# Cutting the last whole output store by columns, and moving two small copies between engines, at the end of a cross-network kernel

## The chip, the cores and the metric

The kernel runs on one core of one Trainium2 chip. The metric is the device time of one execution, in microseconds (us). Executions of one and the same kernel differ by up to about 0.8%, so a kernel is run several times beside the kernel before on the same chip.

## The reference, cut to what matters

```python
B, F, D, L = 16384, 26, 16, 6          # rows; Din = F * D = 416 columns; 6 layers; all bf16
def reference(x0, ws, bs):
    x = x0
    for l in range(L):
        x = x0 * (jnp.einsum('bd,de->be', x, ws[l]) + bs[l]) + x
    return x
```

## The kernel before

The 16384 rows are cut into eight groups of 2048 (groups 0 to 7). A group times a layer is a job, and a job is computed transposed: columns on the 128 partitions, rows along the free dimension. The 416 columns are three tiles of 128 and a "tail" of 32. The DMA engines turn groups 0 to 6 back with DMA transposes before storing them. The last job (group 7, last layer) is different: it is computed in natural layout, and the tile of its input that came last is turned by TensorE.

The output of groups 0 to 6 looks like this:

```python
def output(g):
    def turn(t):                                       # one 128-column tile back to row layout
        add("sp", lambda h: h.dma_start_transpose(ost[:, :, t*P:(t+1)*P], xs[s][:, t*GC:(t+1)*GC]),
            reads=[...], writes=[("ost", t)], lane="ot", batch=g)
    turn(0)
    add("sp", ... dma_start_transpose(ot3, x3s[s3]) ..., writes=["ot3"], lane="ot3", batch=g)
    add("pool", ... tensor_copy(ost[:, :, 384:416], ot3) ...)         # the "spread" of the tails
    turn(1)
    turn(2)
    add("sp", ... dma_start(out[g*GC:(g+1)*GC, :], ost) ...,          # 2048 rows of 832 B
        reads=[("ost", t) for t in range(NT + 1)], lane="out", batch=g)
```

`add` puts an instruction into an engine's queue and works out its waits from what it reads and writes. DMAs are counted on a semaphore for each `lane`. All DMAs of one lane with the same `batch` are one group: whoever waits for one of them waits until the whole group has landed (`val` below is the count at the end of the batch).

```python
for lane, batches in self.lanes.items():
    n = 0
    for k, (key, ops) in enumerate(batches):
        n += 16 * len(ops)
        for op in ops:
            total[id(op)] = (n, ops)
... group = total[id(d)][1];  val = total[id(d)][0]
```

The last job takes the rows in four parts `kk`. For each part it does matmuls (`nat_rows`, `nat_full`), a copy from PSUM by ScalarE (`nat_out`), a multiply and an add on VectorE (`nat_mul`, `nat_add`), and a store. The residual that the add needs is in `x5n`; its third tile is filled by two ScalarE copies, `turned_out(0)` and `turned_out(2)`.

Of the kernel before, what the change touches and what calls it, by code (L numbers as in the profile page):

```python
# [3 lines left out]
P = 128  # L4
# [3 lines left out]
ACT_F = mybir.ActivationFunctionType  # L8
# [13 lines left out]
class Program:  # L22
# [12 lines left out]
    def add(self, eng, fn, reads=(), writes=(), lane=None, batch=None, hold=False, release=False):  # L35
        op = Op(eng, fn, lane, batch)
        deps = {}
        if eng == "pool":
            writes = list(writes) + ["pool"]
        for t in reads:  # L40
            w = self.writer.get(t)
            if w is not None:
                deps[id(w)] = (w, True)
        for t in writes:
            w = self.writer.get(t)
            if w is not None:
                deps[id(w)] = (w, True)
            for r in self.readers.get(t, ()):
                if id(r) not in deps:
                    deps[id(r)] = (r, False)  # L50
        for d, raw in deps.values():
            if d.lane is None and d.eng == eng and lane is None and (eng == "pe" or not raw):
                continue
            op.deps.append(d)
        for t in reads:
            self.readers.setdefault(t, []).append(op)
        for t in writes:
            self.writer[t] = op
            self.readers[t] = []
        if eng == "dve":  # L60
            if hold:
                self.flush()
                self.held = op
            else:
                self.queue[eng].append(op)
                if release:
                    self.flush()
        else:
            self.queue[eng].append(op)
        if lane is not None:  # L70
            batches = self.lanes.setdefault(lane, [])
            if not batches or batches[-1][0] != batch:
                batches.append((batch, []))
            batches[-1][1].append(op)
        return op
# [123 lines left out]
def bass_standalone__cross_network_dcn__recsys_kernel(  # L199
# [6 lines left out]
    B, D = x0.shape  # L206
    L = ws.shape[0]
    NT = 3
    NJ = 4
    GC = NJ * CH  # L210
# [3 lines left out]
    LAST = NG - 1  # L214
# [29 lines left out]
    ts = [nc.alloc_sbuf_tensor(f"ts_{s}", [P, CH], BF16) for s in range(NTS)]  # L244
    ost = nc.alloc_sbuf_tensor("ost", [P, GC // P, D], BF16)
    Tb = ost[:, :, :].rearrange("p a f -> p (a f)")[:, 0:GC]
    ot3 = nc.alloc_sbuf_tensor("ot3", [P, KK, P], BF16)
# [3 lines left out]
    add = pr.add  # L251
# [21 lines left out]
    def take(n):  # L273
        got = [(ring[0] + i) % 8 for i in range(n)]
        ring[0] = (ring[0] + n) % 8
        return got
# [56 lines left out]
    free_x, free_3 = list(range(NXS)), list(range(NX3))  # L333
# [10 lines left out]
    def x3_src(g, l):  # L344
        if l == 0:
            s = slot(g)
            return x0s[s][:, XW:XW + CH], x03_toks(s)
        s = xtail[(g, l)]
        return x3s[s][:, :], [("x3", s)]
# [132 lines left out]
    def tails(batch):  # L482
# [28 lines left out]
        out=ident[:, :], in_=ident[:, :], compare_op=ALU.not_equal, fill=1.0, base=0,  # L511
# [8 lines left out]
    def load_nat(j, k0, k1):  # L520
# [6 lines left out]
        reads=["warm"], writes=["warm"])  # L527
# [18 lines left out]
    def psum_t(b):  # L546
        return psum[:, b * CH:(b + 1) * CH].bitcast(BF16)
# [72 lines left out]
    x0n7, x5n, on = (x0s[s][:, 0:XW + CH].rearrange(view, j=NJ, k=KK) for s in (sn, s5, so))  # L620
# [12 lines left out]
    def output(g):  # L633

        s, s3 = xset[(g, L)], xtail[(g, L)]
        def turn(t):
            add("sp", lambda h: h.dma_start_transpose(
                ost[:, :, t * P:(t + 1) * P], xs[s][:, t * GC:(t + 1) * GC]),
                reads=[("x", s, t, j) for j in range(NJ)], writes=[("ost", t)], lane="ot", batch=g)

        turn(0)
        add("sp", lambda h: h.dma_start_transpose(ot3[:, :, :], x3s[s3][:, :]),
            reads=[("x3", s3)], writes=["ot3"], lane="ot3", batch=g)
        add("pool", lambda h: h.tensor_copy(  # L644
            ost[:, :, NT * P:D].rearrange("p (j k) f -> p j k f", j=NJ),
            ot3[:, :, :].rearrange("p k (j f) -> p j k f", j=NJ)),
            reads=["ot3"], writes=[("ost", NT)])
        turn(1)
        turn(2)
        rows = out[g * GC:(g + 1) * GC, :]  # L650
        o = ost[:, :, :].rearrange("p (j k) f -> p j k f", j=NJ)
        pat = "(j p k) f -> p j k f" if g == 0 else "(j k p) f -> p j k f"
        add("sp", lambda h: h.dma_start(rows.rearrange(pat, j=NJ, k=KK), o),
            reads=[("ost", t) for t in range(NT + 1)], writes=[("out", g)], lane="out", batch=g)
        free_x.append(s)
        free_3.append(s3)

    x5f = x0s[s5][:, 0:XW + CH].rearrange("p (a f) -> p a f", f=D)

# [27 lines left out]
    k = 0  # L687
# [76 lines left out]
    g, l = LAST, L - 1  # L764
    src, stok = x_src(g, l)
    s3, tok3 = x3_src(g, l)
# [9 lines left out]
    def nat_full(kk, j, b, first, ts=range(NT)):  # L776
        for t in ts:
            add("pe", lambda h, t=t: h.matmul(  # L778
                bank(b, n=D), xcol(t, j, kk), wm[l][:, t, :], start=(first and t == 0),
                stop=(not first and t == NT - 1)),  # L780
                reads=[stok(t, j), ("wm", l)], writes=[("ps", b)])
# [10 lines left out]

    def turned_out(j, b):
        t = NT - 1
        add("act", lambda h: h.activation(  # L795
            x5n[:, j:j + 2, :, t * P:NT * P].rearrange("p j k f -> p (j k) f"),
            psum_t(b).rearrange("p (a f) -> p a f", f=P), ACT_F.Copy),
            reads=[("ps", b), "x5 free"], writes=[("x5n", j, t), ("x5n", j + 1, t)])

    def turn_tails(bks):  # L800
        for kk in range(KK):
# [13 lines left out]
    def nat_rows(kk, bks, first=True):  # L815
        for j in range(NJ):
            r, q = quad(g, l, j)
            add("pe", lambda h, j=j, q=q, r=r: h.matmul(  # L818
                bank(bks[j], n=D), x3col(j, kk), w3[l][q, :], start=first, stop=False, tile_position=(r * T32, 0)),
                reads=tok3 + [("w3", l, r)], writes=[("ps", bks[j])])  # L820
        for j in range(NJ):
            r, q = quad(g, l, j)
            add("pe", lambda h, j=j, q=q, r=r: h.matmul(
                bank(bks[j], n=D), ones[q, :], brow[q, :], start=False, stop=False, tile_position=(r * T32, 0)),
                reads=["ones", ("brow", r)], writes=[("ps", bks[j])])

    def nat_out(kk, j, bks):
        extra = x0_all(so) + x03_toks(so) if first_use.pop("on", None) else []
        add("act", lambda h: h.activation(on[:, j, kk, :], bank(bks[j], n=D), ACT_F.Copy),  # L829
            reads=[("ps", bks[j])], writes=extra + [("on", j, kk)])  # L830

    def nat_mul(kk, j, n=2):
        o, x0v = on[:, j:j + n, kk, :], x0n7[:, j:j + n, kk, :]
        toks = [("on", a, kk) for a in range(j, j + n)]
        add("dve", lambda h: h.tensor_tensor(o, o, x0v, ALU.mult),  # L835
            reads=toks + [("n7", a) for a in range(j, j + n)], writes=toks)

    def nat_add(kk, j, n=2):
        o, x5v = on[:, j:j + n, kk, :], x5n[:, j:j + n, kk, :]
        toks = [("on", a, kk) for a in range(j, j + n)]  # L840
        add("dve", lambda h: h.tensor_tensor(o, o, x5v, ALU.add),  # L841
            reads=toks + [("x5n", a, t) for a in range(j, j + n) for t in range(NT + 1)], writes=toks)
# [3 lines left out]
    def nat_store(kk, j0, j1, eng="sp"):  # L846
        dst = out[LAST * GC:B, :].rearrange("(j k p) f -> p j k f", j=NJ, k=KK)[:, j0:j1, kk, :]
        add(eng, lambda h: h.dma_start(dst, on[:, j0:j1, kk, :]),
            reads=[("on", j, kk) for j in range(j0, j1)],
            writes=[("out7", kk, j0)], lane=f"out7_{stores[0]}", batch=0)  # L850
        stores[0] += 1

    a0, a1, a2, a3 = bka = take(NJ)
    b0, b1, b2, b3 = take(NJ)
    bks = {0: bka, 1: [b0, b3, b1, a0], 2: [a1, a2, a3, b2], 3: [b0, b3, b1, a0]}
    for j in range(NJ):
        nat_full(0, j, bks[0][j], True, (0, 1))
    turn_tails([b0, b1, b2, b3])
    nat_rows(0, bks[0], False)
    turn_last(0, b1)  # L860
    turned_out(0, b1)
    for j in range(NJ):
        if j == 2:
            turn_last(2, b2)
        nat_full(0, j, bks[0][j], False, (2,))
        nat_out(0, j, bks[0])
    nat_mul(0, 0)
    nat_add(0, 0)
    nat_mul(0, 2)
    nat_rows(1, bks[1])  # L870
    for j in range(NJ):
        nat_full(1, j, bks[1][j], False)
        nat_out(1, j, bks[1])
        if j == 1:
            turned_out(2, b2)
            nat_mul(1, 0)
            nat_add(1, 0)
    nat_add(0, 2)
    nat_store(0, 0, NJ)
    nat_mul(1, 2)  # L880
    nat_add(1, 2)
    nat_store(1, 0, NJ)
    nat_rows(2, bks[2])
    for j in range(NJ):
# [48 lines left out]
```

## Time and profile before

| what | number | where it is read |
|---|---|---|
| time, three runs | 479.52 us (479.35 to 479.99) | times |
| TensorE busy | 98% of the span | page, part 1 |
| last add on VectorE ends | 474.3 us | timeline |
| DMA engines busy without a break (over 90% from 466.6) | 466.3 to 476.4 us | DMA view of 465 to 478 |
| end of span | 477.8 us | page |

The page of the kernel before says that TensorE is busy all the time (share of the span, and number of instructions):

```profile
PE 469.5 (98%) x3371; PEld 196.3 (41%) x3371; DVE 403.5 (84%) x695; ACT 342.9 (72%) x372; POOL 8.1 (2%) x16
```

That holds for 460 us. The last 20 us have another limit. This is the DMA view of the kernel before, in the window 465 to 478 us, cut into 40 slices of 0.325 us. The first line has the busy share of the DMA engines in tenths, the second what they moved.

```profile
DMA  0000799999999999999999999999999999920000
GB/s 0 0 0 0 271 358 348 358 351 353 343 358 305 351 353 348 338 323 353 330 340 325 340 323 338 333 330 328 330 328 341 325 343 328 320 69 3 0 0 0
DMA packets 4192, 3.41 MB, mean 262 GB/s; under 512 B 96, under 2 KB 4192, under 8 KB 4192
```

From the fifth slice on there is no gap for 10 us. The DMA engines carry 3.41 MB at their full rate, and the last byte comes about 2.4 us after the last arithmetic. Whatever makes arithmetic faster in this stretch changes nothing at the end, unless it lets the bytes start earlier.

They start when group 6 is stored. The timeline of the DMA queue (SP) in the kernel before shows start, duration of the issue, and what is issued; `x2` means two merged issues (the second of this pair starts at 459.95):

```profile
452.58 2.34 SPq L637 DMA_TRANSPOSE ost<-x  x1
454.97 1.44 SPq L642 DMA_TRANSPOSE ot<-x  x1
457.06 6.22 SPq L637 DMA_TRANSPOSE ost<-x  x2
465.38 0.39 SPq L653 DMA_DIRECT2D out_dram<-ost  x1
467.59 6.45 SPq L848 DMA_DIRECT2D out_dram<-x  x4
```

The store at 465.38 waits for the third transpose. That transpose waits for a VectorE add (line 408). The timeline of VectorE and of GpSimd (POOL) around it:

```profile
457.62 0.69 DVE L403 TENSOR_TENSOR tw<-tw,x 128x1024 bf16<-128x1024 bf16 x1
458.22 1.10 DVE L408 TENSOR_TENSOR x<-tw,x 128x1024 bf16<-128x1024 bf16 x1
459.25 0.68 DVE L408 TENSOR_TENSOR x<-tw,x 128x1024 bf16<-128x1024 bf16 x1
...
457.71 1.06 POOL L644 COPY ost<-ot 128x512 bf16<-128x512 bf16 x1 [22.61 <-DMA ot<-x]
```

The add at 458.22 takes 1.10 us where its neighbours take 0.69, and the GpSimd copy lies over its first half. The next add cannot start before it is through; that one ends at 459.92, and the third transpose is issued at 459.95. So these 0.4 us are on the way to the end.

### The profile page before, as it was taken

The numbers are of one execution on the slowest core, as the hardware profiler recorded it, in microseconds if no ns is written. First come the engines' busy times: TensorE is split into PE (matmuls) and PEld (weight loads), VectorE is DVE, ScalarE is ACT, GpSimd is POOL, SyncE is SP. The second block draws the span as 40 slices with busy tenths as digits, with TensorE's granted clock in tenths as the row PEclk, the third lists the DMA queues.
The fourth block names the chain that finished last, engine by engine and source line by source line (L and its number), as shares of the span: only waits on it lengthen the run. The fifth ranks groups of instructions, "written<-read, shape, count | busy, mean of one in ns | idle before, by whom it ended". The sixth has DMA issues, their size and how long they took to land.

```text
span 477.8 us, 8395 instructions
## 1 busy us (share of the span) xinstructions
PE 469.5 (98%) x3371; PEld 196.3 (41%) x3371; DVE 403.5 (84%) x695; ACT 342.9 (72%) x372; POOL 8.1 (2%) x16
## 2 busy tenths in 40 slices
PE   8999999999999999999999999999999999999995
PEld 6344444444444434444444444434444444443342
DVE  2888888888888888898888869888888888888886
ACT  3677777777777777777777777777777777777784
POOL 1000000000000000000000000000000000000000
PEclk9999999999999999999999999999999999999999
DMA  9976930630102377379219931880000138027889
GB/s 230 178 167 148 186 79 1 146 76 1 28 7 46 68 217 157 77 158 242 64 31 208 205 88 29 185 250 0 2 16 21 27 64 229 0 45 161 196 142 285
DMA packets 138315, 53.31 MB, mean 112 GB/s; under 512 B 112282, under 2 KB 137380, under 8 KB 138276
## 3 DMA queue, kind: packets, MB, share of 16 engines
q1 hardware_dynamic: 137528, 52.24, 48.4%
q8 instruction: 26, 0.43, 0.4%
q10 hardware_dynamic: 748, 0.54, 0.4%
q14 instruction: 13, 0.11, 0.1%
HBM read 5.97 MB, written 13.63 MB: 41 GB/s over the span
## 4 chain that ended last, share of the span: by engine, by line
PE 97%; ACT 2%; DVE 1%; issue 0%; POOL 0%; POOLq 0%
PE ps L456 78%; PE ps L477 7%; PE ps L497 7%; PE ps L471 1%; PE ps L778 1%; PE ps L561 1%; ACT x L829 1%; PE ps L488 1%; PE ps L541 1%; ACT x L795 0%; DVE x L841 0%; DVE x L835 0%; ACT x L565 0%; PE ps L789 0%; PE ps L818 0%
## 5 line engine op out<-in xcount | busy, mean ns | idle before, releaser
L394 ACT ACTIVATE tw<-ps,bias 128x1024 bf16<-128x1024 f32 (+1 forms) x295 | 299.8, 1071 | 119.8 <-PE ps L477 75.7
L456 PE MATMUL ps<-x,wm 128*128 128x512 bf16 x1692 | 380.1, 380 | 0.0
L456 PEld LDWEIGHTS ps<-x,wm 128*128 128x128 bf16 x1692 | 159.2, 98 | 213.7 <-issue 29.1
L403 DVE TENSOR_TENSOR tw<-tw,x 128x1024 bf16<-128x1024 bf16 (+1 forms) x285 | 192.4, 683 | 53.6 <-ACT tw L394 53.4
L408 DVE TENSOR_TENSOR x<-tw,x 128x1024 bf16<-128x1024 bf16 (+1 forms) x285 | 182.5, 681 | 0.0
L477 PE MATMUL ps<-x,w 32*128 32x512 bf16 x512 | 39.2, 379 | 0.0
L497 PE MATMUL ps<-x,wm 128*32 128x512 bf16 x564 | 33.0, 380 | 0.0
L434 ACT ACTIVATE ts<-ps,bias 128x512 bf16<-128x512 f32 x47 | 28.8, 701 | 0.0
L438 DVE TENSOR_TENSOR x<-ts,x 128x512 bf16<-128x512 bf16 x47 | 18.6, 417 | 3.5 <-DMA x<-x 3.5
L497 PEld LDWEIGHTS ps<-x,wm 128*32 128x32 bf16 x564 | 13.8, 96 | 17.6 <-issue 5.3
L477 PEld LDWEIGHTS ps<-x,w 32*128 32x128 bf16 x512 | 7.8, 92 | 27.6 <-issue 27.5
L436 DVE TENSOR_TENSOR ts<-ts,x 128x512 bf16<-128x512 bf16 x47 | 18.5, 417 | 0.0
L644 POOL COPY ost<-ot 128x512 bf16<-128x512 bf16 x7 | 6.6, 947 | 445.7 <-DMA ot<-x 445.7
L778 PE MATMUL ps<-wm,x 128*128 128x416 bf16 x48 | 9.4, 340 | 0.0
L568 DVE COPY x<-ps 128x512 bf16<-128x512 bf16 x4 | 1.7, 424 | 9.0 <-PE ps L561 9.0
L829 ACT ACTIVATE x<-ps 128x416 bf16<-128x416 f32 x16 | 7.8, 522 | 1.1 <-PE ps L778 1.0
L565 ACT ACTIVATE x<-ps 128x512 bf16<-128x512 bf16 x8 | 4.2, 598 | 6.0 <-PE ps L561 6.0
L835 DVE TENSOR_TENSOR x<-x,x 128x832 bf16<-128x832 bf16 (+1 forms) x9 | 4.9, 540 | 2.1 <-ACT x L829 2.1
L778 PEld LDWEIGHTS ps<-wm,x 128*128 128x128 bf16 x48 | 4.4, 98 | 4.1 <-issue 1.0
L488 PE MATMUL ps<-x,w 32*32 32x512 bf16 x188 | 5.9, 374 | 0.0
L471 PE MATMUL ps<-x,w 32*32 32x512 bf16 x208 | 5.6, 385 | 0.0
L561 PE MATMUL ps<-ident,x 128*128 128x128 bf16 x64 | 5.3, 242 | 0.3 <-ACT x L565 0.3
(36 smaller groups left out, 36.7 us busy)
## 6 DMA issues: line engine op xcount, KB each, us to landing
out_dram<-ost SPq DMA_DIRECT2D x7, 1664.0 KB, 6.8
x<-in_x_dram SPq DMA_DIRECT2D x7, 416.0 KB, 7.9
x<-x SPq DMA_DIRECT2D x24, 96.0 KB, 2.2
wm<-in_ws_dram SPq DMA_DIRECT2D x5, 312.0 KB, 3.3
x<-x SPq DMA_DIRECT2D x22, 64.0 KB, 2.0
out_dram<-x SPq DMA_DIRECT2D x3, 416.0 KB, 5.8
x<-ost SPq DMA_DIRECT2D x28, 32.0 KB, 2.3
x<-x SPq DMA_DIRECT2D x24, 32.0 KB, 1.9
```

The costliest lines, as they stand in the source:

```text
L394: add("act", lambda h, a=a, w=w, b0=b0: h.activation(tw[r][:, a * CH:(a + w) * CH], psum[:, b0 * CH:(b0 + w) * CH], ACT_F.Identity, bias=b ...
L403: add("dve", lambda h, a=a, e=e: h.tensor_tensor(tw[r][:, a * CH:e * CH], tw[r][:, a * CH:e * CH], x0s[s0][:, i * GC + a * CH:i * GC + e * ...
L408: add("dve", lambda h, a=a, e=e: h.tensor_tensor(xs[so][:, i * GC + a * CH:i * GC + e * CH], tw[r][:, a * CH:e * CH], src(i, a, e), ALU.ad ...
L434: add("act", lambda h: h.activation(ts[r][:, :], bank(b), ACT_F.Identity, bias=bias[:, 3, l:l + 1], scale=1.0), reads=[("ps", b), "bias"], ...
L436: add("dve", lambda h: h.tensor_tensor(ts[r][:, :], ts[r][:, :], x03, ALU.mult), reads=[("ts", r)] + tok0, writes=[("ts", r)], release=True)
L438: add("dve", lambda h: h.tensor_tensor(x3s[so][:, :], ts[r][:, :], res, ALU.add), reads=[("ts", r)] + rtok, writes=[("x3", so), ("x3", so, ...
L456: add("pe", lambda h, t=t, j=j: h.matmul(bank(banks[j]), wm[l][:, t, ecols], src(t, j, j + 1), start=(first and t == 0), stop=(not first a ...
L477: add("pe", lambda h, q=q, j=j, r=r: h.matmul(bank(banks[j]), w3[l][q, ecols], src[q, :], start=first, stop=not first, tile_position=(r * ...
L488: add("pe", lambda h, l=l, b=b, s3=s3, ri=ri, qi=qi, ro=ro, qo=qo: h.matmul(psum[qo, b * CH:(b + 1) * CH], w3[l][qi, NT * P:D], s3[qi, :], ...
L497: add("pe", lambda h, t=t, j=j, src=src, l=l, b=b, ro=ro, qo=qo: h.matmul(psum[qo, b * CH:(b + 1) * CH], wm[l][:, t, NT * P:D], src(t, j, ...
L778: add("pe", lambda h, t=t: h.matmul(bank(b, n=D), xcol(t, j, kk), wm[l][:, t, :], start=(first and t == 0), stop=(not first and t == NT - 1)),
L829: add("act", lambda h: h.activation(on[:, j, kk, :], bank(bks[j], n=D), ACT_F.Copy), reads=[("ps", bks[j])], writes=extra + [("on", j, kk)])
```

## The change

The intent: let 256 of the 416 columns of group 6 be stored while the third transpose is still running; take the spread of the tails off GpSimd, where it holds up VectorE; give one of two residual copies to VectorE, so that ScalarE can start sooner on the outputs of the last job.

```diff
@@ output(g), group 6 only (g == LAST - 1)
-        add("pool", ... spread ...)
+        if g < LAST - 1:
+            spread("pool")
         turn(1)
         turn(2)
-        add("sp", ... store of all 416 columns, reads all of ost ...)
+        if g < LAST - 1:
+            store(g, 0, D, range(NT + 1))
+        else:
+            store(g, 0, 2 * P, (0, 1))            # columns 0..255, 512 B pieces
@@ before the last job
+    spread("act")
+    store(LAST - 1, 2 * P, D, (NT - 1, NT))       # columns 256..415, 320 B pieces
@@ turned_out(j, b)
-        add("act", ... activation(dst, sp_, Copy) ...)
+        if j:  add("act", ... activation(dst, sp_, Copy) ...)
+        else:  add("dve", ... tensor_copy(dst, sp_) ...)
@@ last job: order on ACT and DVE
-    nat_mul(0, 0); nat_add(0, 0); nat_mul(0, 2)     # turned_out(2), nat_add(0, 2), nat_store(0) come later
+    turned_out(2, b2)
+    for j in (0, 2): nat_mul(0, j); nat_add(0, j)
+    nat_store(0, 0, NJ)
     ... (part 1 in the plain order too; further cuts)
```

More of the change, by code (lines that the diff above doesn't have):

```diff
@@ L643, in output, with spread, store @@
             reads=[("x3", s3)], writes=["ot3"], lane="ot3", batch=g)
-        add("pool", lambda h: h.tensor_copy(
-            ost[:, :, NT * P:D].rearrange("p (j k) f -> p j k f", j=NJ),
-            ot3[:, :, :].rearrange("p k (j f) -> p j k f", j=NJ)),
-            reads=["ot3"], writes=[("ost", NT)])
+        if g < LAST - 1:
+            spread("pool")
         turn(1)
         turn(2)
-        rows = out[g * GC:(g + 1) * GC, :]
-        o = ost[:, :, :].rearrange("p (j k) f -> p j k f", j=NJ)
+        if g < LAST - 1:
+            store(g, 0, D, range(NT + 1))
+        else:
+            store(g, 0, 2 * P, (0, 1))
+        free_x.append(s)
+        free_3.append(s3)
+    def spread(eng):
+        dst = ost[:, :, NT * P:D].rearrange("p (j k) f -> p j k f", j=NJ)
+        sp_ = ot3[:, :, :].rearrange("p k (j f) -> p j k f", j=NJ)
+        kw = dict(reads=["ot3"], writes=[("ost", NT)])
+        if eng == "act":
+            add("act", lambda h: h.activation(dst, sp_, ACT_F.Copy), **kw)
+        else:
+            add(eng, lambda h: h.tensor_copy(dst, sp_), **kw)
+    def store(g, f0, f1, ts):
+        rows = out[g * GC:(g + 1) * GC, f0:f1]
+        o = ost[:, :, f0:f1].rearrange("p (j k) f -> p j k f", j=NJ)
         pat = "(j p k) f -> p j k f" if g == 0 else "(j k p) f -> p j k f"
         add("sp", lambda h: h.dma_start(rows.rearrange(pat, j=NJ, k=KK), o),
-            reads=[("ost", t) for t in range(NT + 1)], writes=[("out", g)], lane="out", batch=g)
-        free_x.append(s)
-        free_3.append(s3)
+            reads=[("ost", t) for t in ts], writes=[("out", g, f0)], lane="out", batch=g)
     x5f = x0s[s5][:, 0:XW + CH].rearrange("p (a f) -> p a f", f=D)
@@ L794, in turned_out @@
         t = NT - 1
-        add("act", lambda h: h.activation(
-            x5n[:, j:j + 2, :, t * P:NT * P].rearrange("p j k f -> p (j k) f"),
-            psum_t(b).rearrange("p (a f) -> p a f", f=P), ACT_F.Copy),
-            reads=[("ps", b), "x5 free"], writes=[("x5n", j, t), ("x5n", j + 1, t)])
+        dst = x5n[:, j:j + 2, :, t * P:NT * P].rearrange("p j k f -> p (j k) f")
+        sp_ = psum_t(b).rearrange("p (a f) -> p a f", f=P)
+        kw = dict(reads=[("ps", b), "x5 free"], writes=[("x5n", j, t), ("x5n", j + 1, t)])
+        if j:
+            add("act", lambda h: h.activation(dst, sp_, ACT_F.Copy), **kw)
+        else:
+            add("dve", lambda h: h.tensor_copy(dst, sp_), **kw)
     def turn_tails(bks):
@@ L866, in bass_standalone__cross_network_dcn__recsys_kernel @@
         nat_out(0, j, bks[0])
-    nat_mul(0, 0)
-    nat_add(0, 0)
-    nat_mul(0, 2)
+    turned_out(2, b2)
+    for j in (0, 2):
+        nat_mul(0, j)
+        nat_add(0, j)
+    nat_store(0, 0, NJ)
     nat_rows(1, bks[1])
@@ L873, in bass_standalone__cross_network_dcn__recsys_kernel @@
         nat_out(1, j, bks[1])
-        if j == 1:
-            turned_out(2, b2)
-            nat_mul(1, 0)
-            nat_add(1, 0)
-    nat_add(0, 2)
-    nat_store(0, 0, NJ)
-    nat_mul(1, 2)
-    nat_add(1, 2)
+        if j % 2:
+            nat_mul(1, j - 1)
+            nat_add(1, j - 1)
     nat_store(1, 0, NJ)
```

## The prediction

The text says "rings" for the 16 DMA engines.

> **What bounds it now.** For 460 us TensorE does (98% busy on the page). The change touches only the last 20 us, and there the DMA rings finish last. In the DMA view of 465 to 478 us they go from idle to over 90% busy at 466.3 and stay there, at 320 to 358 GB/s, until 476.4; the span ends at 477.8. They carry 3.41 MB: the store of group 6 (1664 KB, issued 465.38, timeline) and five stores of group 7. Arithmetic ends at 474.3; the rings are then 2 us behind. So the end is the issue of group 6's store + about 0.9 + bytes / rate + about 1.4.
>
> **What releases that store.** Three transposes into `ost`, issued 452.58, 457.06, 459.95; the third lands about 465.3. It starts when the VectorE add ending 459.93 lets it. That add ran 1.10 us instead of 0.69, and the GpSimd copy of the tails (457.71, 1.06 us) lies over it: the lock on the shared port pair that the Trainium skill ("SBUF — State Buffer", section "SBUF: two separate sides") describes; this trace agrees, with 0.41 us.
>
> **What the change does.**
> 1. Spread to ScalarE: VectorE's chain from 457.7 on, and with it the third transpose, runs about 0.45 us earlier. On ScalarE the spread costs about 0.6 us (128x512 copies from PSUM: 0.60), inside the 0.67 us it idled before 460.57. Gain 0.45 us, on the critical path.
> 2. Split store. By the code the first part does not leave after two transposes: all three count on one semaphore, as one batch, and a wait is for the whole batch. The built order shows that wait at the first part, none at the second. Nothing is won; the parts leave at about 464.9 and 465.3. But rows of 832 B become 512 B and 320 B. Group 0, stored in 3328 B pieces, moved at about 400 GB/s, 832 B rows at about 350. My estimate from these two: 6 ns per piece and engine over a straight line, 128 more pieces each, +0.8 us of ring time. The Trainium skill ("DMA: Bandwidth & Descriptors", "Specifications") gives 512 B as the least size for full rate, with read-modify-write below; 40% of the bytes are below now. No trace shows it for stores; it could add another 1 us.
> 3. One copy of turned columns to VectorE (about 0.7 us, estimated from the 0.42 us copy of half the size, into 1.36 us of idle) takes 1.02 us from ScalarE; the first group-7 store leaves at about 465.8 instead of 467.59, TensorE ends about 0.7 us earlier. But these stores queue behind full rings: worth nothing at the end.
>
> Sum: -0.45 + 0.8 + part of 1 = a little slower, near nothing on 479.5.
>
> **Predicted:** 479.8 us, range 478.6 to 481.3. Faster by over 2%: 0.01; within 2%: 0.98; slower by over 2%: 0.01.
>
> **What would show it.** Last arithmetic 0.5 to 0.9 us earlier; the add at 458.2 back at 0.69 us; first part issued at 464.9, after the third transpose has landed, second 0.4 us later; rings full from there to the end, at a lower rate (about 300 GB/s) in the first 5 us; the last landing longer after the last store's issue than before.
>
> **What would make it wrong.** If small pieces cost nothing, it is 0.4 us faster. If the third transpose, which stops moving from 462 to 463.5 for no reason I can name, runs through when it starts earlier, 1.5 us more is gained. If the first part does leave after two transposes, its 1.05 MB fills idle stretches and the end comes up to 2 us earlier, until arithmetic bounds it.

## The result, and the profile after

| | median | runs |
|---|---|---|
| before | 479.75 us | 6 (479.35 to 481.69) |
| after | 480.83 us | 6 (480.29 to 482.41) |

The ratio is 1.0015 (95% interval 0.9991 to 1.004). A ratio here is the mean time of one kernel's runs over that of the other's of the same rounds, so not quite the ratio of the medians. The difference is within 2%, and on these runs alone its sign is not settled. The traces show more.

The page after, as before:

```profile
PE 462.7 (97%) x3317; PEld 196.0 (41%) x3371; DVE 403.7 (84%) x696; ACT 342.3 (72%) x372; POOL 7.1 (1%) x15
```

(Some matmul records are missing from this trace: 3317 matmuls against 3371 weight loads. TensorE's instructions are the same in number.)

The DMA view of the kernel after in the window 465 to 478 us:

```profile
DMA  0089999999999999999999999999999999999100
GB/s 0 0 260 320 317 317 315 312 265 257 340 312 292 261 255 237 243 236 246 241 251 256 305 328 330 333 340 328 333 328 338 323 335 325 333 338 297 41 0 0
DMA packets 6256, 3.41 MB, mean 262 GB/s; under 512 B 2160, under 2 KB 6256, under 8 KB 6256
```

The same 3.41 MB start 0.65 us earlier (0.27 of it because this whole trace runs that much ahead, see below) and end later. For 3 us they move at about 310 GB/s, then for 3 us at about 245, and only then at the old 330. Before there were 4192 packets, now there are 6256, of which 2160 are under 512 B.

The timeline after: the DMA queue, then lines of VectorE and ScalarE:

```profile
456.79 4.40 SPq L637 DMA_TRANSPOSE ost<-x  x2
464.71 1.92 SPq L670 DMA_DIRECT2D out_dram<-ost  x2
466.67 6.85 SPq L866 DMA_DIRECT2D out_dram<-x  x4
...
457.95 1.28 DVE L408 TENSOR_TENSOR x<-tw,x 128x1024 bf16<-128x1024 bf16 x2
...
459.47 0.67 ACT L661 ACTIVATE ost<-ot 128x512 bf16<-128x512 bf16 x1
...
472.53 0.38 DVE L859 TENSOR_TENSOR x<-x,x 128x416 bf16<-128x416 bf16 x1
```

Two adds now take 1.28 us together, so the one that was held up is back at 0.69 (the neighbour's lock is gone). Both parts of the store are issued together at 464.71, not one of them 3 us ahead. The last add ends at 472.9, where it ended at 474.3 before.

**The tail.** A whole span is made of a start, a body and a tail. Between the first evacuation of a batch of the 32 left-over columns (line 434, at about 20 us) and the first matmul of the last job, the body lasts 437.91 or 437.92 us in the traces of all eight kernels here that leave it alone. The start varies from trace to trace, between 20.1 and 22.9 us, also where nothing in it was changed; that is most of the scatter. The tail does not see it. Each tail below comes from a single trace, so its scatter was not measured by repeating; the one pair of kernels that should have the same tail, before and rows_split, differs by 0.02 us. The two TensorE lines that it is counted from, before and then after:

```profile
458.72 1.57 PE L778 MATMUL ps<-wm,x 128*128 128x416 bf16 x8
```

```profile
458.45 1.57 PE L793 MATMUL ps<-wm,x 128*128 128x416 bf16 x8
```

So the tail is 477.8 - 458.72 = 19.1 us before and 478.5 - 458.45 = 20.0 us after. The change loses 0.9 us, and it does so although arithmetic ends 1.15 us earlier in it (14.46 us into the tail instead of 15.61).

### The profile page after: what moved, and what is told of

Same layout as the page of the kernel before. It is cut to its first block, busy times and chain, and to the rows that moved or that the text cites. A ratio compares the mean times of both kernels' runs of the same rounds, so it can differ in the third digit from the quotient of the medians.

```text
span 478.5 us, 8341 instructions
## 1 busy us (share of the span) xinstructions
PE 462.7 (97%) x3317; PEld 196.0 (41%) x3371; DVE 403.7 (84%) x696; ACT 342.3 (72%) x372; POOL 7.1 (1%) x15
## 4 chain that ended last, share of the span: by engine, by line
PE 93%; DVE 2%; ACT 2%; issue 1%; POOL 0%; POOLq 0%
PE ps L456 75%; PE ps L477 7%; PE ps L497 6%; ACT tw L394 2%; PE ps L793 1%; PE ps L471 1%; DVE x L408 1%; PE ps L561 1%; DVE tw L403 1%; PE ps L541 1%; PE ps L488 1%; DVE x L859 0%; DVE x L853 0%; ACT x L565 0%; PE ps L804 0%
## 5 line engine op out<-in xcount | busy, mean ns | idle before, releaser
L456 PE MATMUL ps<-x,wm 128*128 128x512 bf16 x1638 | 372.2, 380 | 5.6 <-issue 3.7
L438 DVE TENSOR_TENSOR x<-ts,x 128x512 bf16<-128x512 bf16 x47 | 18.8, 422 | 3.6 <-DMA x<-x 3.6
```

Source lines behind the costliest of these rows:

```text
L438: add("dve", lambda h: h.tensor_tensor(x3s[so][:, :], ts[r][:, :], res, ALU.add), reads=[("ts", r)] + rtok, writes=[("x3", so), ("x3", so, ...
L456: add("pe", lambda h, t=t, j=j: h.matmul(bank(banks[j]), wm[l][:, t, ecols], src(t, j, j + 1), start=(first and t == 0), stop=(not first a ...
```

## The experiments

Twelve kernels were run. Each "total" is the ratio to the kernel before in the same rounds; each "tail" comes from the one profiled run, counted as above.

| kernel | total (95% interval) | tail, us | last arithmetic, us into the tail |
|---|---|---|---|
| before | 1 | 19.11 | 15.61 |
| after | 1.0015 (0.9991 to 1.004) | 20.00 | 14.46 |
| split_only | 1.0028 (1.0016 to 1.004) | 20.34 | 15.62 |
| rows_split | 1.0011 (0.9995 to 1.0026) | 19.09 | 15.61 |
| cols_equal | 1.0034 (1.0011 to 1.0058) | 20.5 | 15.62 |
| one_store | 0.9991 (0.9975 to 1.0007) | 18.58 | 14.45 |
| no_copy | 1.0027 (1.0008 to 1.0047) | 20.2 | 15.40 |
| own_sem | 0.9987 (0.9974 to 1.0) | 18.55 | 14.45 |
| after_moved | 1.0033 (1.0013 to 1.0052) | 18.8 | 14.45 |
| one_store_moved | 1.0005 (0.9982 to 1.0027) | 18.70 | 14.45 |
| own_sem_moved | 1.0013 (0.9991 to 1.0035) | 18.97 | 14.45 |
| own_sem_quiet | 0.9999 (0.9975 to 1.0023) | 17.97 | 14.45 |
| one_store_quiet | 1.001 (0.9987 to 1.0032) | 17.89 | 14.45 |
| own_sem_quiet_no_copy | 1.0019 (0.9995 to 1.0043) | 17.95 | 15.40 |

The tails can be checked against the totals: the change of tail and body together, over 479.3 us, should lie in the interval of the total. It does for every kernel but after_moved (see 7).

The theory to be tested was: the DMA engines bound the end; the change starts their work 0.4 us earlier and makes it longer by cutting its pieces. The rivals: the loss comes from elsewhere, or from the mere number of transfers; and arithmetic counts after all.

### 1. The split alone (split_only)

The kernel before, with this in `output(6)` and nothing else:

```diff
-  dma_start(out[rows, 0:416], ost[..., 0:416])
+  dma_start(out[rows, 0:256], ost[..., 0:256]);  dma_start(out[rows, 256:416], ost[..., 256:416])
```

> The kernel before with nothing but the store of group 6 cut into columns 0..255 and 256..415, both behind all three transposes. Theory (the end is set by the rings, and small pieces move slower): the parts leave where the one store left (about 465.4 in the earlier trace's time), 512 B pieces move at about 315 GB/s and 320 B pieces at about 245, the last byte comes 1.0 to 1.4 us later than before, total +1.0 to +1.4 us (ratio 1.002 to 1.003). Rival (the small loss of the change comes from elsewhere, from group-7 stores that start earlier, or is noise): same as before, within 0.3 us.

Measured: total 1.0028, median 480.75 against 479.27 us; tail 20.34, 1.23 us over before. The DMA view of split_only from 465 to 478 us shows both rates:

```profile
GB/s 0 0 0 27 306 315 325 310 320 302 236 291 336 314 281 261 252 240 234 246 238 245 249 275 307 330 333 325 340 328 328 335 335 328 335 328 335 330 249 15
```

The theory's numbers were met. The split is the loss, and it is more than the net loss of the change.

### 2. Two transfers of whole rows (rows_split)

```diff
-  one store of 2048 rows
+  two stores of 1024 rows each, pieces still 832 B
```

> The kernel before with the store of group 6 cut by rows into two halves, all pieces still 832 B. Theory (it is the size of the pieces that costs): same as before within 0.3 us, rate about 350 GB/s in both halves. Rival (a second transfer on the queue costs by itself): about 1.3 us slower, as with the split by columns.

Measured: tail 19.09, before 19.11. The total, 1.0011, does not exclude 1. A second transfer costs nothing by itself; the size of the pieces does.

### 3. Other pieces (cols_equal)

```diff
-  one store of columns 0..415
+  columns 0..207 and 208..415, pieces of 416 B
```

> The kernel before with the store of group 6 cut into two column parts of 208, pieces of 416 B. From the traces so far: 832 B pieces move at about 350 GB/s (38 ns each and ring), 512 B at 315 (26 ns), 320 B at 243 (21 ns). If the time of a piece is a fixed part and a part per byte (6.5 ns + 38 ns per 1000 B), 416 B take 22 ns, 300 GB/s, and the tail is 0.8 us longer than before; if pieces under 512 B pay an extra 2.5 ns, as the 320 B ones seem to, 25 ns, 270 GB/s, and 1.5 us longer. [...]

Measured: tail 20.5, 1.4 us over before; 1.0034 in total. With the spacing of packets of one size (the middle 80% of them, times 16 engines) from the DMA records of the traces, the four sizes are:

| piece | ns for one piece on one engine | all 16 engines |
|---|---|---|
| 832 B (before) | 38.6 | 345 GB/s |
| 512 B (split_only) | 26.9 | 305 GB/s |
| 416 B (cols_equal) | 25.5 | 261 GB/s |
| 320 B (split_only) | 20.9 | 245 GB/s |

A row of 832 B takes 38.6 ns whole and 26.9 + 20.9 = 47.8 ns in two pieces. Each engine has 2048 / 16 = 128 rows, so the split costs 128 x 9.2 ns = 1.18 us, against 1.23 us in the tail. A line through 832 and 512 B (8 ns and 37 ns per 1000 B) would give 23.4 and 19.9 ns for the two small sizes; they lie 2.1 and 1.0 ns above. The Trainium skill ("DMA: Bandwidth & Descriptors", section "Specifications") gives 512 B as the least size for line rate, with a read-modify-write below. In these stores there is a small extra below 512 B, and the larger part of the cost is a fixed time per piece that is there above 512 B too. This division is an estimate: whole-row stores in the traces of before and after have spacings from 38.3 to 41.9 ns, and 41.9 instead of 38.6 in the same sum would leave about 3 ns for each of the two. A split by columns also changes where in a row of the output the pieces start; size and place were not tried apart. Nothing like a halved rate was seen: the lowest is 245 GB/s. What the split costs in the tail depends on none of this.

### 4. One store, the rest of the change kept (one_store)

```diff
-  store(g, 0, 2 * P, (0, 1))  ...  store(LAST - 1, 2 * P, D, (NT - 1, NT))
+  store(LAST - 1, 0, D, range(NT + 1))          # once, after the spread
```

> The changed kernel with the store of group 6 left whole (832 B pieces), spread on ScalarE and copy on VectorE kept. Theory: the VectorE add is not held up, third transpose and store 0.4 us earlier than before, rings full from there at about 340 GB/s, end 0.4 us earlier than before (ratio about 0.999) and about 1.2 us earlier than the changed kernel. Rival (splitting costs nothing): like the changed kernel, 1.0015 of before.

Measured: tail 18.58, 0.53 us under before and 1.42 us under after; total 0.9991, median 479.15 against 479.27. So the spread on ScalarE, together with the copy on VectorE (about 0.2 us of it, if the next experiment is taken at its word), is worth about what the lock had cost, and the split costs the rest. The Trainium skill ("SBUF — State Buffer", section "SBUF: two separate sides") says that VectorE and GpSimd share a pair of ports under an exclusive lock; the traces agree with it in this place, with 1.10 us for the add beside the GpSimd copy and 0.69 us without it. Beside the spreads of three earlier groups in the trace of before (at 206, 254 and 434 us) one VectorE operation each takes 1.10 us too.

### 5. The copy undone (no_copy)

```diff
-  turned_out(0) on VectorE; multiplies, adds and stores in the new order
+  turned_out(0) and turned_out(2) on ScalarE, everything in the order of before
```

> The changed kernel with both copies of the turned columns on ScalarE again, and multiplies, adds and stores of group 7 in the order of before; split store and ScalarE spread kept. Theory (rings bound the end): last arithmetic 0.5 to 1 us later than in the changed kernel, the total the same within 0.3 us. Rival (the arithmetic chain counts): 0.5 to 1 us slower than the changed kernel.

Measured: last arithmetic 0.95 us later than in the changed kernel (15.40 against 14.46), tail 0.2 us longer. The copy does its work and the end hardly sees it, since the DMA engines are behind. The totals of the two kernels (1.0027 and 1.0015) come from different rounds, and their intervals overlap.

### 6. What the split was meant to be (own_sem)

The prediction had read from the code that the first part waits for all three transposes. One word makes it wait for two:

```diff
-            ..., writes=[("ost", t)], lane="ot", batch=g)
+            ..., writes=[("ost", t)], lane="ot6" if (g, t) == (LAST - 1, NT - 1) else "ot", batch=g)
```

> The changed kernel with a semaphore of its own for the third transpose of group 6, so that the first part waits for two transposes alone. Theory: first part issued about 3.3 us earlier than in the changed kernel (about 461.4), its 1.05 MB moves in stretches where the rings were idle; the second part leaves as in the changed kernel; last byte 2 to 3 us earlier than in the changed kernel, total 1.5 to 2.5 us under before (ratio 0.995 to 0.997), with the last store's landing shrunk to about 2.5 to 3 us. Rival (the first part already left as early as it can, or its traffic delays the third transpose by as much): no better than the changed kernel.

Measured: first part issued at 460.88. Tail 18.55, 1.45 us under after, but only 0.56 us under before and no better than one_store; total 0.9987. Expected were 1.5 to 2.5 us under before: most of the gain is missing. The DMA queue of own_sem, and its DMA view in the window 461 to 465 us (slices of 0.1 us), show where. The last fence has the bytes of before in the same window:

```profile
460.88 4.09 SPq L670 DMA_DIRECT2D out_dram<-ost  x2
465.02 7.21 SPq L866 DMA_DIRECT2D out_dram<-x  x4
```

```profile
DMA  9999999000000000000299999999999999999999
GB/s 218 384 197 197 125 28 5 0 0 0 0 3 8 8 10 8 10 10 10 54 284 287 289 287 294 292 287 290 326 343 364 338 348 343 364 338 348 343 364 338
...
q8 instruction: 1, 0.02, 1.7%
```

```profile
GB/s 0 51 179 210 366 200 202 169 56 18 0 0 0 0 0 0 0 8 8 8 10 10 10 8 13 223 289 292 292 289 287 287 287 292 289 292 294 292 178 0
```

The first part is issued at 460.88, and from 461.5 to 462.9 almost nothing moves, although a transpose and a store are queued. At 463.0 the transpose goes on, and the store's bytes follow it from 463.8. The same hole is in the traces of before and after, at almost the same distance from the first matmul of the last job. It was the pause that the prediction could not name. A first part that starts 1.5 us late just earns back what its small pieces cost: its store is done 12.11 us into the tail, one_store's 12.08.

The line `q8 instruction: 1` in that window is a clue. It counts one packet of 16 KB, with the name "instruction". Before has 26 of them in its span. The Trainium skill ("Perfetto Trace Analysis", section "Per-instruction lifecycle: what the profiler-reported window actually captures") says that instructions have 64 bytes; 16 KB are then 256 instructions, and TensorE starts 256 instructions between two such packets on average in the trace. In all eight traces described so far, the last of them lies 2.2 to 4.2 us into the tail, across the hole. The records of the DMA packets (times from the first matmul of the last job):

```
kernel      16 KB packet on q8    longest 256 B transpose packet beside it
before      +2.73 to +4.02        1.84 us
after       +3.06 to +4.13        1.61 us
own_sem     +3.05 to +4.13        1.66 us
```

Half of all 256 B packets in the trace of before take 0.018 us or less, and 99 in 100 less than 0.06 us. This gave a new theory: a fetch of TensorE instructions holds up a DMA transpose in flight.

The packet records hold more of the same. Packets of 256 B that took over 1 us come in clusters. After the first 10 us of the span the 14 traces have 68 such clusters, and 67 of them lie beside a 16 KB packet (in before at 12.9, 266.5, 301.3 and 461.7 us). But the link is not strict: a cluster at 8.1 us in before has no such packet beside it, and a transpose that began during the fetch at 203.7 us had no packet over 0.6 us.

### 7. The fetch moved (after_moved, one_store_moved, own_sem_moved)

Three late groups of sixteen 32x32 matmuls are written as four 32x128 each, with the same result. That is 72 TensorE instructions fewer, counting weight loads, and every fetch after them comes 72 instructions later.

```diff
+    plain = [n for n in sorted(mode) if mode[n] == "F1"][-3:]
-            rows32(g, l, i, banks, False, mode[n] == "F1")
+            rows32(g, l, i, banks, False, mode[n] == "F1" and n not in plain)
```

> The changed kernel (both parts behind all three transposes) with 72 fewer TensorE instructions. Theory: like the one-store pair, both parts 1.2 to 1.7 us earlier, total 1.0 to 1.6 us under the changed kernel, so about 0.9985 of before; and still about 1.2 us over the one-store kernel without the pause, because of the small pieces. Rival: same as the changed kernel.

> The one-store kernel with three late TensorE groups of sixteen 32x32 matmuls written as four 32x128 matmuls each: 72 fewer TensorE instructions, so that the last 16 KB fetch of TensorE instructions, seen in all traces so far at 461.1 to 463.8 in the middle of the third transpose, comes about 3 us later. Theory (that fetch holds a transpose in flight, and makes the pause of about 1.5 us): the fetch starts after 463.5, the transpose runs through, the store is issued 1.2 to 1.7 us earlier than in the one-store kernel, total 1.0 to 1.6 us under it. Rival (the pause belongs to the transpose itself or to its issue): pause and store stay where they were, total within 0.3 us.

> The kernel with an own semaphore for the third transpose, and 72 fewer TensorE instructions as in the one-store pair. Theory: no pause, the first part's bytes move from about 462.3 instead of 463.2, the second part leaves about 1.5 us earlier, the rings catch up with arithmetic, which then bounds the end; total 0.6 to 1.3 us under the kernel with the pause, about 0.996 of before. Rival: pause stays, no gain.

Measured: the fetch moved by 2 to 4 us in all three, as it must if it belongs to TensorE's instructions, and the hole in the third transpose was gone in all three. This is the DMA view of one_store_moved from 461 to 465 us:

```profile
DMA  9999999999999999999999996100800000000000
GB/s 226 279 272 261 212 212 220 212 192 236 212 205 228 212 218 220 218 218 218 210 195 187 210 223 128 23 0 0 164 0 0 0 0 0 0 0 0 0 0 0
```

The last transpose packet ended 4.97 us into the tail instead of 5.62 (one_store_moved), 4.62 instead of 5.77 (after_moved) and 4.98 instead of 5.78 (own_sem_moved). That part of the theory is shown.

The gain at the end was there in the tail of after_moved (18.8, 1.15 us under after) and missing in the other two (18.70 against 18.58, and 18.97 against 18.55). Both were misses. The DMA view of own_sem_moved from 465 to 478 us tells why:

```profile
DMA  9999999999999999999999999998100000000000
GB/s 249 290 280 248 264 249 243 240 239 248 237 261 248 319 326 322 325 338 320 336 330 333 328 330 340 328 333 238 41 23 20 20 20 3 0 0 0 0 0 0
```

At 474.1 the work is done but for a trickle of 20 GB/s, and the trickle lasts 1.6 us. 20 GB/s is a sixteenth of 330: one engine is late, alone. In this kernel the fetch came at +6.81 to +7.81, while all 16 engines were storing. The fetch itself moves 16 KB at about 16 GB/s, the work of one engine for about 1 us. An engine that loses 1 us while all are full has no idle time in which to catch up. In one_store_moved the fetch (+5.25 to +6.55) ran just over the start of the store (+6.46), and the last byte came 1.1 us after the engines ceased to be full. In after_moved it ended at +6.07 as the store began (+6.06), and this gap was 0.4 us, as it is in the trace of before. The records name no engine, so that the late one is the one that fetched is an inference from these rates and times.

In totals these kernels gained less still: the rewritten groups made the body 0.29 us longer, and the runs scatter. The total of after_moved was a miss as well: about 0.9985 was expected and 1.0033 measured (1.0013 to 1.0052), while its tail and body give no change against before. Its one profiled run is the fastest of its six; why the others are slower stays open.

### 8. The fetch put before the third transpose (own_sem_quiet, one_store_quiet, own_sem_quiet_no_copy)

```diff
+    f1 = [n for n in sorted(mode) if mode[n] == "F1"]
+    plain = {n: NJ for n in f1[:8]}; plain[f1[8]] = 1      # 198 TensorE instructions fewer
```

> The kernel with an own semaphore for the third transpose, and eight early TensorE groups of sixteen 32x32 matmuls as four 32x128, a ninth in part: 198 fewer TensorE instructions, so that the last 16 KB fetch of TensorE instructions falls into the idle stretch of the rings at about 457.0 to 458.2 and none comes after. Counted from the first matmul of the last job to the end of the span (before 19.11 us, the same kernel with the fetch in the third transpose 18.55, with the fetch among the stores 18.97). Theory (a fetch costs about 1 us of one ring wherever the rings are full, by a pause of all 16 or by one that ends late; only in an idle stretch it is free): no pause, no late ring, last byte at about +16.5, end at +17.3 to +17.8, total about 1.5 us under before. Rival (the late bytes after +16.1 belong to something else): end stays at 18.5 to 19.0.

> The one-store kernel with the same 198 fewer TensorE instructions. Theory: the store is issued about 1.5 us earlier than in the one-store kernel and no ring is late; rings full until about +16.3, end at +17.5 to +17.9 from the first matmul of the last job (one-store kernel 18.58): nearly as good as with the early first part, since the missing 5 us of ring time are about made up. Rival: stays at 18.5.

> The first kernel of this set with both copies of turned columns on ScalarE and the order of before. Theory (with the rings no longer 2 us behind, arithmetic bounds the end, so the copy on VectorE now counts): last arithmetic 0.95 us later than with the copy and the end 0.7 to 1.0 us later. Rival (the copy never counts): same end within 0.2 us.

Measured: one fetch fewer in the whole span. The line of the page of own_sem_quiet:

```profile
q8 instruction: 25, 0.41, 0.4%
```

The last fetch came 2.45 us before the tail (2.47 and 2.33 in the others). That is 0.7 us earlier than aimed, and it still met transposes, earlier ones (longest packets 1.3 to 1.7 us). Even so the one store left 5.40 us into the tail instead of 6.15. No engine was late at the end. The tails are 17.97, 17.89 and 17.95, the shortest of all and 1.1 to 1.2 us under before. one_store_quiet is just within its 17.5 to 17.9; own_sem_quiet missed its 17.3 to 17.8 by 0.2. Three things follow. With the fetch out of the way, the whole store ends as early as the split one with its early start, as expected. The copy on VectorE still made no difference (17.95 without, 17.97 with), so the expectation for it, 0.7 to 1.0 us, was wrong: without the copy the DMA engines were full until 16.89 us into the tail and with it until 16.41, but the last bytes came at 17.00 and 16.92. Why the earlier arithmetic was not turned into earlier last bytes was not followed further. And the totals show no gain, since the rewritten groups cost 1.15 us in the body (439.07 us instead of 437.92, and 439.29 in own_sem_quiet_no_copy), as much as the tail won.

No kernel beats the one before clear of noise. own_sem comes nearest: 0.9987, with an interval that ends at 1.0.

## Why the prediction was right or wrong

**The time: 479.8 us predicted, 480.83 measured, in the range of 478.6 to 481.3.** Both "within 2%" and "a little slower" held; the second is shown by the tail (20.0 against 19.1 us) and not by the totals alone. The range says little, since it is about as wide as the scatter of before's own six runs (479.35 to 481.69); the terms of the sum are the better test.

**The DMA engines bound the end: right.** Arithmetic ended 1.15 us earlier and the end came later. no_copy moved arithmetic by 0.95 us and the tail by 0.2 us.

**Spread to ScalarE, gain 0.45 us: right.** The add was back at 0.69 us. (The text takes the slow add for the one that releases the transpose; it is the one before that, and the delay is passed on.) Relative to the first matmul of the last job, the third transpose was issued 0.41 us and the store 0.40 us earlier; one_store put the gain at the end at 0.53 us. The spread took 0.67 us on ScalarE, inside the idle time.

**The first part waits for all three transposes: right.** Both parts were issued together, and own_sem, where it waits for two, issued it 3.45 us earlier relative to the first matmul of the last job.

**Small pieces, +0.8 us and part of 1: the term that was mis-sized.** The prediction took 6 ns for an additional piece, from 3328 B and 832 B pieces, and hedged with a possible read-modify-write. Measured was 9.2 ns for a row in two pieces, 1.18 us in all, and 1.2 to 1.4 us in the tails. The straight line from larger pieces gave too little fixed time for a small one. The hedge, a possible read-modify-write of up to 1 us, was large enough for the rest, but that is luck: no such cost of its own was shown. The predicted median is 0.3 us over before, and the tail lost 0.9.

**The copy on VectorE, "worth nothing at the end": right within 0.2 us.** Its details were less so. Arithmetic ended 1.15 us earlier, not 0.5 to 0.9 (nor did this gain help once the fetch was out of the way: own_sem_quiet_no_copy). The first store of group 7 left at 466.67 and not at 465.8: its data were ready at 465.2, but the queue was still issuing the second part, an issue that took 1.48 us instead of 0.4.

**The pause in the third transpose: named as open, and it stayed.** "If the third transpose [...] runs through when it starts earlier" did not come true, since the pause follows TensorE's instructions and not the transpose's issue.

## What to carry to other kernels

The end of this kernel is a full DMA queue, and two things moved it: when the bytes start, and how long each piece takes. A fetch of instructions beside the transpose or among the stores also went with a later end. Where a kernel ends like this, count the pieces a split makes before counting what it overlaps. A finer dependency helps only if the semaphore behind it is as fine: check the wait that is actually built. And compare stages with a stretch of the trace that noise at the start can't reach, when the effect is smaller than the scatter of whole runs.

## What the Trainium skill lacked or had wrong

- No page that was searched says what a fetch of instructions does to data in flight. The fetch itself is described in "Runtime: NRT & Kernel Launch", section "Instruction fetch mechanics" (blocks of 16 KiB, 256 instructions, over a DMA queue), and "DMA: Bandwidth & Descriptors" lists a queue row for refills among those that share the DMA engines. Here a 16 KB fetch of TensorE instructions went with a stop of a DMA transpose for about 1.5 us (single 256 B packets took 1.6 to 1.8 us), did not visibly slow a plain load of 832 B pieces as a whole (351 GB/s during a fetch at 315.4 us in the trace of before), and was followed by one late engine (20 GB/s for 1.6 us) where all 16 were full. Why a transpose stops on all engines at once was not found.
- "DMA: Bandwidth & Descriptors", section "Specifications", has a threshold of 512 B with a read-modify-write below. Stores from SBUF with row pieces of 832, 512, 416 and 320 B took 38.6, 26.9, 25.5 and 20.9 ns for a piece: no jump at 512 B, and by estimate a fixed time per piece with 1 to 2 ns more under 512 B. That page does have a fixed overhead per packet, in its section "Why small descriptors are slow (HBM only)"; what it lacks is a measured time for such stores on trn2.
